# Eight of sixteen filter-spreading transfers on ScalarE's queue, and a new order, in a fused state-space convolution and gated MLP

## The chip, the cores and the metric

The kernel runs on one core of a Trainium2 chip. The metric is the device time of one execution, in microseconds; each kernel is run several times and the median is quoted. The profile is one execution taken by the hardware profiler, and its times count from the start of its span.

The engines are called by the profile's names: PE is TensorE (PEld its weight loads), DVE is VectorE, ACT is ScalarE, POOL is GpSimd, and SP is SyncE, which here does nothing but issue transfers.

## The reference, cut to what matters

The input `x` is 2048 positions by 640 channels. After a layer normalisation, `xn` goes through two branches, and the output is the sum of `x` and both.

```python
xn = layernorm(x)
# branch A: a long convolution per channel d, its filter K made from 128 complex modes n
P = exp(dt * (A_re + 1j * A_im) * l)                 # 640 x 128 x 2048
K = einsum('dn,dnl,dn->dl', C, P, dt * B).real       # 640 x 2048
y = irfft(rfft(pad(K)) * rfft(pad(xn.T)))[:, :2048].T + xn * Dskip
# branch B: gated MLP with a mixing over positions
z = gelu(xn @ w_in)                                  # 2048 x 1728
z1, z2 = z[:, :864], layernorm(z[:, 864:])
g = w_sp @ z2 + b_sp[:, None]                        # 2048 x 2048 times 2048 x 864
out = x + y + (z1 * g) @ w_out                       # 864 x 640
```

## The kernel before, in words

**Stages.** Everything is in one program, in which the two branches are interleaved.

- *Start (0 to about 90 us).* `x` and `w_in` are loaded. DVE and ACT normalise `x` into `xn`, which also goes to the DRAM buffer `xn_scratch`. PE makes `xn @ w_in` (tags `mm1b` and `mm1a`: 432-wide matmuls, ten for each of 32 row blocks), and ACT evicts each with a gelu. The second half of `w_in`'s columns (`WINB`) is used first. DVE computes the statistics of `z2`; each of the 16 `z2` blocks is then normalised either on ACT or on DVE.
- *Filter (about 90 to 200 us).* The class `Kgen` makes the filter `K` for 20 chunks of 32 channels (`NCH`, `CH`), in two parts of ten chunks. For each chunk PE makes phases (`kpe`), ACT turns them into sines in two instructions (tag `ktrig`, function `trig`), DVE multiplies magnitudes (`mags`) and products (`products`), and PE contracts them over the modes (`contract`, 64 small matmuls on 24 columns). `kg.trigs[c]` is the last sine instruction of chunk `c`; other work is tied to these. There are three buffers for the sines (`NTR`). Each part's magnitudes need exponentials on ACT (`exps`), which need another activation table than the sines. Between the chunks PE works at the mixing `w_sp @ z2` (`mm2`), whose `w_sp` tiles come by transposing transfers; DVE gates the result (`gate`), and it goes to the DRAM buffer `zg_scratch`.
- *Convolution (about 195 us to the end).* The class `Conv` transforms input and filter in two stages of matmuls (`stage1`, `stage2`), multiplies them on DVE (tag `pw`), and transforms back (`inverse1`, then `inv2`), once for each of the two parts. The input of the first transform, `TLU`, is loaded by `load_u` from `xn_scratch` in eight transfers of 320 KB. The large constant of the second stage is `C2`. In between and after it, PE does the last product, `mm3`, on tiles of `zg_scratch` that transposing transfers bring (tag `zgt`).

**The fill.** A part's filter lies in `K2` with the values that the reference's bf16 positions call for, and has to be spread into `TLK`, the operand of `stage1`. `expand` writes `K2` to the DRAM buffer `k2d_scratch` (four stores), reads back four larger pieces, and then 16 small ones of 20 KB: eight for positions kept exactly, eight for those rounded to two (`EXACT` and `HALVES`; line 1324). Twelve copies on DVE or ACT (tag `spread`) spread the rest. The fill is done twice, once for each part. All its transfers are on SP's queue.

**What sets the order.** The program is first recorded as a list of operations. `Builder.schedule` then places them one by one on their engines: it goes by estimated durations, by the length of the work that hangs on each operation, and by an added figure for each group of operations (`SHIFT`, a long table). Some copies may go to ACT or to DVE, and the planner picks. What results is a fixed order for each engine and each queue, with semaphore waits where operations touch the same memory. `B.after(op, earlier)` only keeps an operation from being placed before another; it puts no wait into the program. An engine, or SP's queue, does its list in order: what stands behind a waiting entry waits too. Where tiles lie in SBUF is another table (`OFFSETS`). Tiles that aren't needed at the same time overlap, and the overlap makes waits.

The lines that the change touches besides these tables:

```python
XOT = 10
WOT = 12
UOT = 14
    cv.load_const("c2", "C2", kg.trigs[17])
    cv.load_u([kg.trigs[UOT + m // 2] for m in range(8)])
            B.dma(WINB, winv[:, :, FH:FF])
```

So the eight loads of `load_u` are tied to the sines of chunks 14 to 17, `C2` to chunk 17, and `w_out` to chunk 12.

Of the kernel before, what the change touches and what calls it, by code (L numbers as in the profile page):

```python
# [65 lines left out]
class Builder:  # L66
# [304 lines left out]
    def dma(self, out, in_, q="sp", wait=()):  # L371
        nb = self._dma_bytes(out)
        run = min(self._run(out), self._run(in_))
        per = 0.077e-3 if min([128] + [a.ap[0][1] for a in (out, in_) if 'DRAM' not in str(a.space).upper()]) <= 32 and run > 2048 else 0.037e-3 if run < 6000 else 0.045e-3
        op = self._add(q, lambda e: e.dma_start(out, in_), [in_] + list(wait), [out], is_dma=True, dur=0.55, lat=nb / run * (10e-3 + per * run) / 16)  # L375
        op.late = self.late.get(self.tag, 0.0)
        op.npk = nb / run / 16
        return op
# [337 lines left out]
class Psum:  # L716
# [25 lines left out]
FF = 1728  # L742
FH = 864
# [8 lines left out]
CH = 32  # L752
# [17 lines left out]
XOT = 10  # L770
WOT = 12
UOT = 14
OUTQ = (("sp",) * 4,) * 4 + (("sp", "pool", "sp", "pool"), ("sp", "act", "sp", "act"))
SHIFT = [
    1461.6, -117.7, 5299.6, -320.3, 1656.3, -585.1, 1763.6, 26.1, 1267.1, 880.0, -633.4, -370.4, 42.1, -1405.2, -471.9, 240.0,
    254.6, 1219.7, 333.5, -1999.5, 1976.3, 2197.4, 40.4, -90.3, -103.2, 540.3, 3080.4, 42.1, 38.8, 2850.1, 556.2, -367.7, 67.3,
    5571.0, -530.7, 952.0, -24.5, 338.5, 6324.0, 537.2, 302.2, 180.6, -957.6, 1643.2, 16.8, 902.2, -1600.9, 605.1, -802.3,
    2031.4, -1306.0, -780.7, -671.9, 112.0, -3008.2, -525.0, 1040.2, 862.9, 1287.1, 984.6, 0.0, -64.7, -959.6, -9.0, -1054.5,
    -2630.8, -2537.1, -2991.9, -1011.8, -3926.2, -591.7, -6744.4, -9.0, 25.9, -7345.2, -1133.1, -9424.9, -1929.4, 627.4, -364.0,
    965.9, 496.7, 629.4, -110.8, -121.3, -759.7, -1177.4, 480.5, -1197.3, -3403.7, -447.7, 898.1, 1345.4, -2969.0, -1517.5, 0.0,  # L780
    -3435.2, -1369.8, -37.9, 6726.1, 1236.6, -140.5, 449.9, -632.2, 1096.4, 284.8, 301.9, 276.3, 842.6, 378.2, 12361.1, 2383.3,
    4141.9, 0.0, -1.6, -165.8, 1279.3, 48.4, 2124.7, 2354.1, 906.1, 2654.6, -806.7, -347.3, -1862.7, -471.1, -522.2, -1067.9,
    -415.0, 2743.0, 1234.3, -270.9, -752.3, 0.0, 229.7, -988.3, 1179.3, 2749.5, 422.5, -55.8, -40.7, -68.1, -811.0, 0.0, 1089.6,
    1757.0, 1526.0, 2103.2, -69.7, 626.4, -30.5, -3352.9, -188.7, 1862.3, -2385.7, -1180.5, -549.1, -5568.3, 3140.0, -636.8,
    -226.7, -4354.1, -17.8, -184.5, 53.9, -9607.2, -2.9, -5759.3, -1188.1, -260.2, 1.3, -657.7, -2203.7, -424.7, -732.5, -2.6,
    -1322.0, 1.1, -489.2, -2.2, -2.6, 92.4, 1408.5, -2763.9, -641.9, -12.6, 66.3, 2712.2, -1338.6, -449.1, 162.2, -1878.5,
    1052.8, 986.9, 0.0, -1173.7, -951.0, 1307.7, -89.6, 1382.7, -4152.3, 6.1, 942.4, -13.1, 0.0, 2750.8, -383.8, 450.2, -592.9,
    -1973.8, 1396.3, 341.7, -2846.0, -307.2, 2653.6, 1018.7, -127.0, 1161.5, -341.3, -0.2, -519.7, 0.0, -2933.3, 992.3, -2932.9,
    1285.4, 933.9, -233.4, -4592.7, 850.7, -588.8, -606.5, -1083.9, 863.2, -449.4, -1858.1, -1.0, -436.2, -541.3, 978.0, -8.2,
    153.5, 929.5, -4177.6, -1.0, -742.2, -810.7, -1914.2, -970.0, -4.6, 868.9, -5270.0, -0.1, 14.4, -364.3, 227.7, -3.8, 2351.5,  # L790
    996.3, -6118.5, 1072.5, -4920.9, -10.5, 989.9, 2108.7, -4207.9, 19.9, -650.3, -2.3, 1697.9, 812.0, -48.7, 16.3, 0.0, -316.5,
    964.2, 2.4, 5.1, 12756.5, 413.6, -63.9, -29.5, -247.6, 12.2, 1000.8, 11416.5, -1091.2, 3120.4, 0.0, 219.7, 4899.7, -1039.5,
    -18.9, 4401.0, -2120.8, -14.1, 3471.9, 134.1, 1185.1, 7.0, 61.4, 7.0, -458.7, 67.2, 1741.9, 3459.0, 68.9, 1615.7, -607.8,
    -48.2, 1376.1, -152.7, 1791.3, 1014.0, 0.0, -1221.0, -500.9, 146.5, 7270.1, 231.7, -225.5, -476.5, -1970.4, 4833.2, -1016.4,
    76.0, -958.1, 206.8, -1937.6, 247.3, 0.0, 5.1, -3306.0, -1829.8, 196.8, 1528.0, 578.8, 1283.1, -501.8, -1621.3, 2897.0,
    7359.7, 1164.5, 3170.6, 9585.4, 696.7, 1828.4, 62.5, 2076.9, 1961.4, 1622.8, 3367.0, 2213.6, 1983.8, 16237.3, 2883.0,
    3106.7, 2690.4, 5604.1, 3820.4, 2156.5, 2325.2, 6606.1, 4254.2, 17981.2, 7.3, 5268.5, -674.7, -197.5, 2.0, 275.0, 8441.8,
    1305.0, 7453.6, 1391.6, 5133.7, 6281.3, 1384.9, 0.0, -324.3, 4083.8, 6831.6, 1385.9, 645.6, 430.0, 2533.1, -2947.5, 1282.5,
    807.3, -985.8, 2140.1, 1551.5, 464.9, -32.2, 3938.7, -84.9, -667.9, 190.1, 1220.1, 1192.0, 565.5, 1690.5, -869.4, 595.3,
    -704.9, 1174.8, -126.1, 11.4, 2116.3, 0.0, -997.8, 3517.0, 61.0, 1088.4, 1.6, 209.1, 10.9, -2456.1, -7207.6, -1631.5,  # L800
    -2836.8, -1735.7, -1533.6, -2236.7, 2.0, -1781.5, 1615.3, -2828.3, 1612.6, 1.8, 498.8, -3860.5, 4550.3, 416.1, 1572.6,
    -200.4, 881.8, -129.8, 319.4, -635.6, -45.7, -1084.3, 684.5, -830.4, -904.9, 58.0, -5231.7, -9.6, -70.8, 54.4, -1.7, 1.7,
    197.8, -193.2, -808.6, 39.4, -1904.6, -564.9, -1099.6, -21.6, -2289.8, -981.9, 957.2, 64.0, 5.7, 140.6, -1217.1, -166.9,
    10728.7, -230.1, 2524.4, 2209.7, 2255.4, 2580.2, -406.2, 1829.0, 972.4, 2954.1, 12199.2, 1506.0, 7180.5, 2130.2, 883.2,
    645.0, 6101.4, 1578.5, 847.9, -410.2, 3588.0, -2096.9, 4371.8, 5289.6, 1519.0, 2347.8, 1268.9, 98.9, 1.7, 2484.5, 3068.8,
    1414.5, 1969.4, 1062.7, 2271.3, 1196.4, 2147.0, 11592.3, 1106.4, 2144.0, 3679.9, -496.8, -7.5, 251.2, 17.1, -12.1, 153.6,
    769.9, 2667.8, 2251.3, -1391.0, 980.8, 996.5, 1113.4, 1225.2, -647.7, -349.9, 1919.7, -565.0, -129.2, -3495.3, -838.1,
    1603.9, -2605.8, -2855.8, 3148.0, -1020.3, 177.0, -2319.3, -4039.8, -3072.6, 531.6, 2401.0, 325.9, -3196.0, 1351.6, -2042.4,
    -3195.4, 2784.7, 1092.8, -260.7, -3300.8, -1668.5, -0.7, -28.4, -5227.0, 785.7, 23.5, 13.4, 0.0, 1159.2, 391.1, 8974.4,
    991.1, 965.3, -7163.2, -49.9, -844.4, 455.0, 96.6, 1.8, -2806.9, -328.1, -295.1, -18.8, -1970.3, -95.4, 1187.4, 102.0,  # L810
    -561.1, 62.5, -3884.6, -261.6, -5032.3, -332.0, -878.8, 207.4, -2.9, -728.4, -89.8, 62.0, 337.2, 0.0, 3155.1, 1202.6,
    3304.3, -211.8, 1376.2, 1544.4, 4613.0, 1618.6, 855.2, 1948.7, 2402.5, 1219.8, -1015.0, 2111.1, 3970.0, 7.0, -1728.5,
    1520.9, -194.9, -327.8, -2723.9, 1962.7, -1508.7, 1013.1, 2968.0, 117.0, -1067.3, 857.2, -3517.0, -397.6, -2125.0, -2912.3,
    1654.7, -50.0, 1368.4, -188.2, -716.4, 1993.7, 1409.8, -17.9, 1083.9, -465.4, 52.4, -105.8, -981.2, -2476.5, 989.7, 0.7,
    -112.8, 1859.9, -218.8, 1528.8, 2260.2, 283.0, -1286.4, -561.2, -2070.2, 510.3, -819.9, 220.5, 43.5, 146.7, -2443.4, 1339.6,
    -2363.1, -970.2, -4841.4, -878.2, -3598.7, -1020.2,
# [9 lines left out]
NTR = 3  # L826
NF = 3
# [3 lines left out]
    "BSB": 0, "RS2": 0, "Tpp": 0, "WOUT": 0, "YT0": 0, "NM2": 64, "ONE": 64, "MV2": 128,  # L831
    "WAV0": 256, "LDP": 320, "DTB": 384, "ST2": 1536, "MV": 1664, "RS": 1792, "NM": 1856, "YT1": 1920,
    "CEXP": 2560, "ST": 2624, "Twim": 2624, "WAV1": 2624, "LDT": 3392, "IDENT": 5184, "TAL1": 5440, "DTP": 6720,
    "TAL0": 8960, "XO": 8960, "Ttr": 10240, "WDP": 10240, "Tw2": 15360, "Twre": 17920, "MF": 19200, "UP0": 19200,
    "RG": 20736, "Tt4": 21312, "WS1": 21312, "XN": 21312, "Tt3": 23872, "Tth": 26432, "UP1": 29440, "TR2": 29504,
    "PC": 31552, "GT0": 34752, "K20": 38976, "RAW": 41792, "WS0": 44288, "Twab": 51456, "TR1": 52480, "RF": 57728,
    "X": 59520, "Z2": 60160, "V2": 70400, "CI": 87808, "KB0": 88320, "WINB": 88320, "WS2": 90240, "LFG0": 98432,
    "TLU": 98432, "Z": 98432, "PLB1": 108672, "KB2": 118912, "Y1K0": 118912, "Y1U0": 118912, "Y1K1": 120832, "Y1U1": 120832,
    "LFG1": 124672, "MG": 132352, "WINA": 132352, "TR0": 134464, "BSP": 141312, "K21": 141376, "PLB0": 141376, "KB1": 145600,
    "TLK": 147520, "XNT": 157376, "WS3": 157760, "C2": 165952, "DSKM": 178240, "W1U": 178560, "Z1": 179072, "GT1": 207744,  # L840
    "W1": 211968,
}
# [940 lines left out]
```

## Time and profile before

Before: 350.3 us, the median of three runs (348.77 to 352.11). The profiled span is 348.8 us.

| Engine | busy us | share of the span |
|---|---|---|
| PE | 317.8 | 91% |
| DVE | 263.2 | 75% |
| ACT | 229.2 | 66% |
| POOL | 17.9 | 5% |

A row of the windows (first us, last us, length) gives each engine's busy time and count of instructions in that stretch; PEclk is the share of full clock that TensorE was granted, and the DMA share is the mean busy share of the core's 16 DMA engines. It can pass 1 because packets overlap. A row of the waits gives who waited for whom, the total in us, how often, and the longest. A row of a timeline merges like instructions in sequence: start, time from the first to the last, and in brackets the idle time before them with its releaser. Rows with "q" behind the engine's name (SPq) are the issuing of transfers, and their time is the queue's, not the transfer's.

### The profile page before, as it was taken

The page shows a single profiled execution, that of the slowest core. Times are in us where ns is not written, and L with a number is a line of the kernel's source. Part 1 is how long each engine was busy: PE and PEld are TensorE (multiplying, and loading weights), DVE is VectorE, ACT ScalarE, POOL GpSimd, SP SyncE. Part 2 cuts the span into 40 slices and gives each one's busy share as a digit, 9 for nine tenths or more (in the row PEclk, how much of TensorE's full clock was granted, in tenths as well). Part 3 has the DMA queues.
Part 4 walks back from the last instruction along what each step waited for, and adds up shares of the span by engine and source line. Part 5 has one row for each costly group of instructions (what it writes and reads, how often), then busy time and mean ns, then how long its engine had stood idle before and what let it go on. Part 6 is the DMA issues. An engine that isn't in the chain of part 4 may idle for free.

```text
span 348.8 us, 9905 instructions
## 1 busy us (share of the span) xinstructions
PE 317.8 (91%) x4282; PEld 214.1 (61%) x4282; DVE 263.2 (75%) x502; ACT 229.2 (66%) x266; POOL 17.9 (5%) x34
## 2 busy tenths in 40 slices
PE   3899998999999999999999399999959999999972
PEld 2454566766466555565656267776638877659862
DVE  5998999998699998389899726649933396883282
ACT  3579984799566679875697127838835877446541
POOL 4111000211100000000000000000000200000001
PEclk9999999999999999999999969999998999999975
DMA  7994566454991647678999998896344869200047
GB/s 213 391 341 157 83 194 167 110 106 93 166 172 45 105 89 118 112 187 188 85 60 136 141 276 201 171 189 112 64 71 116 178 133 214 84 3 2 2 109 197
DMA packets 101700, 48.67 MB, mean 140 GB/s; under 512 B 82137, under 2 KB 99514, under 8 KB 101146
## 3 DMA queue, kind: packets, MB, share of 16 engines
q1 hardware_dynamic: 100824, 45.07, 63.0%
q0 software_dynamic: 448, 2.79, 4.1%
q8 instruction: 33, 0.54, 0.7%
q10 hardware_dynamic: 386, 0.20, 0.2%
q14 instruction: 9, 0.07, 0.1%
HBM read 18.47 MB, written 11.61 MB: 86 GB/s over the span
## 4 chain that ended last, share of the span: by engine, by line
PE 56%; SPq 14%; ACT 13%; DVE 7%; DMA 5%; issue 2%; POOL 0%; POOLq 0%; DVEq 0%
PE ps L341 55%; SPq L375 11%; ACT arena L263 10%; DVE arena L273 4%; ACT L263 3%; SPq L382 3%; DMA arena<-xn_scratch 2%; DMA arena<-in_B_w_in_dram 2%; DVE arena L1099 1%; DVE arena L285 1%; DMA arena<-zg_scratch 1%; DVE arena L304 1%; PE ps L348 0%; DVE ps L297 0%; DVE arena L280 0%
## 5 line engine op out<-in xcount | busy, mean ns | idle before, releaser
L341 PE MATMUL ps<-arena 128*24 128x33 bf16 (+11 forms) x4222 | 314.6, 269 | 22.9 <-DMA arena<-xn_scratch 6.1
L341 PEld LDWEIGHTS ps<-arena 128*128 128x128 bf16 (+5 forms) x4222 | 210.0, 114 | 124.1 <-issue 25.3
L263 ACT ACTIVATE arena<-ps 128x1024 bf16<-128x1024 f32 (+6 forms) x184 | 173.8, 972 | 108.4 <-PE ps L341 97.6
L273 DVE TENSOR_TENSOR arena<-arena 128x128 bf16<-128x128 bf16 (+12 forms) x199 | 121.2, 646 | 13.4 <-ACT arena L263 10.5
L304 DVE CAST arena<-ps 128x1024 bf16<-128x1024 f32 (+2 forms) x28 | 32.5, 1171 | 25.5 <-PE ps L341 21.2
L273 DVE TENSOR_TENSOR arena<-ps,arena 128x320 bf16<-128x320 f32 (+3 forms) x42 | 22.9, 561 | 23.7 <-PE ps L341 23.5
L263 ACT ACTIVATE arena<-arena 128x320 bf16<-128x320 f32 (+10 forms) x65 | 34.6, 590 | 3.3 <-DVE arena L273 2.9
L1513 DVE BATCH_NORM_STATS2 arena<-arena 128x6 f32<-128x320 bf16 (+1 forms) x64 | 30.1, 535 | 3.2 <-DMA arena<-in_A_u_dram 3.1
L285 DVE SCALAR_TENSOR_TENSOR arena<-ps,arena 128x432 bf16<-128x432 f32 x32 | 21.1, 662 | 11.3 <-PE ps L341 9.5
L263 ACT ACT_TABLE_LOAD x17 | 21.8, 1283 | 2.0 <-issue 1.8
L280 DVE TENSOR_SCALAR arena<-arena 128x544 bf16<-128x544 bf16 (+5 forms) x43 | 13.2, 317 | 1.0
L375 POOL DMA_DIRECT2D arena<-in_A_u_dram x8 | 4.1, 514 | 190.4 <-PE ps L341 183.2
L271 POOL TENSOR_TENSOR arena<-arena 128x4 f32<-128x4 f32 (+2 forms) x10 | 9.8, 977 | 62.1 <-DVE arena L280 62.1
L313 DVE TENSOR_SCALAR arena<-arena 128x864 bf16<-128x864 bf16 (+1 forms) x19 | 8.1, 479 | 0.1
L348 PE MATMUL ps<-arena 128*128 128x128 bf16 x60 | 6.0, 238 | 1.7 <-DVE arena L280 1.7
L348 PEld LDWEIGHTS ps<-arena 128*128 128x128 bf16 x60 | 4.6, 107 | 4.0 <-DVE arena L280 2.1
L304 DVE COPY arena<-arena 32x960 bf16<-32x960 bf16 (+4 forms) x14 | 4.6, 375 | 0.1
L285 DVE SCALAR_TENSOR_TENSOR arena<-arena 128x4 f32<-128x4 f32 (+4 forms) x14 | 4.6, 328 | 0.1
L375 POOL DMA_DIRECT2D out_dram<-arena x2 | 1.0, 501 | 70.6 <-DVE arena L273 70.6
L1099 DVE RECIPROCAL arena<-arena 128x640 f32<-128x640 f32 x1 | 4.2, 4153 | 0.0
L1515 DVE BATCH_NORM_AGGREGATE arena<-arena 128x2 f32<-128x12 f32 x32 | 3.9, 169 | 0.1
L304 DVE CAST arena<-arena 128x1280 bf16<-128x1280 f32 (+1 forms) x4 | 2.6, 660 | 0.1
(11 smaller groups left out, 6.5 us busy)
## 6 DMA issues: line engine op xcount, KB each, us to landing
arena<-arena SPq DMA_DIRECT2D x12, 360.0 KB, 6.2
zg_scratch<-arena SPq DMA_DIRECT2D x16, 216.0 KB, 2.4
xn_scratch<-arena SPq DMA_DIRECT2D x4, 640.0 KB, 5.5
arena<-in_A_u_dram POOLq DMA_DIRECT2D x8, 320.0 KB, 6.6
arena<-xn_scratch SPq DMA_DIRECT2D x8, 320.0 KB, 8.2
arena<-in_B_w_in_dram SPq DMA_DIRECT2D x2, 1080.0 KB
arena<-in_A_u_dram SPq DMA_DIRECT2D x3, 640.0 KB
out_dram<-arena SPq DMA_DIRECT2D x16, 120.0 KB, 2.1
```

Source lines behind the costliest of these rows:

```text
L263: return e.activation(out, in_, func, bias=bias, scale=scale)
L271: return self._add(q, lambda e: e.tensor_tensor(out, in0, in1, op), [in0, in1], [out], dur=d, port=True)
L273: return self._add(q, lambda e: e.tensor_tensor(out, in0, in1, op), [in0, in1], [out], dur=self._dve_cost("tt", out, [in0, in1]), port=port)
L280: return self._add(q, lambda e: e.tensor_scalar(out, in0, s1, s2, op0, op1), self._aps(in0, s1, s2), [out], dur=self._dve_cost("ts", out, ...
L285: return self._add("dve", lambda e: e.scalar_tensor_tensor(out, in0, scalar, in1, op0, op1), self._aps(in0, scalar, in1), [out], dur=self. ...
L304: "dve": (lambda e: e.tensor_copy(out, in_), self._dve_cost("ts", out, [in_]))}
L313: "dve": (lambda e: e.tensor_scalar(out, in_, scale, bias, ALU.mult, ALU.add), self._dve_cost("ts", out, [in_]) + 0.11)}
L341: op = self._add("pe", lambda e: e.matmul(out, lhsT, rhs, start=start, stop=stop, **kw), [lhsT, rhs], [out], dur=d)
L348: op = self._add("pe", lambda e: e.transpose(out, in_, ident), [in_, ident], [out], dur=0.09, lat=0.3)
L375: op = self._add(q, lambda e: e.dma_start(out, in_), [in_] + list(wait), [out], is_dma=True, dur=0.55, lat=nb / run * (10e-3 + per * run) ...
L382: return self._add(q, lambda e: e.dma_start_transpose(out, in_), [in_], [out], is_dma=True, xbar=True, dur=1.3 if nb < 400000 else 2.6, la ...
L1513: B.generic("dve", (lambda e, c=c: e.bn_stats(st[:, a, c, :], src[:, a, w * c:w * c + w])), [src[:, a, w * c:w * c + w]], [st[:, a, c, :]] ...
```

## The change

The eight small `HALVES` transfers of each fill are issued from ACT's queue (`EXQ`), so that SP's queue has fewer to issue. `load_u`, `C2` and `w_out` are tied to earlier chunks (12 to 15, 15 and 10). `WINB` is loaded in two halves, one for each half of a block's matmuls. The rows of the filter table run the other way, so that the pieces to be read lie at regular places; the magnitudes' plane order follows, and their last two small products become one of 192 and one of 64 elements in place of two of 128. The planner's estimates for a transfer's issue and for the time to landing of `load_u` change, and both tables (`SHIFT`, `OFFSETS`) are new, so that the order changes throughout. The two tables and the reordered constants are left out of the diff here.

```diff
-        op = self._add(q, lambda e: e.dma_start(out, in_), [in_] + list(wait), [out], is_dma=True, dur=0.55, lat=nb / run * (10e-3 + per * run) / 16)
+        op = self._add(q, lambda e: e.dma_start(out, in_), [in_] + list(wait), [out], is_dma=True, dur=0.66 if self.tag == "expand" else 0.57, lat=nb / run * (10e-3 + per * run) / 16)
...
+EXQ = "act"
+XOT, WOT, UOT, C2T = 10, 10, 12, 15
...
-ROWS = [2 * r for r in range(16)] + [0, 2, 0, 2, 0, 2, 4, 6]
+ROWS = [30 - 2 * r for r in range(16)] + [2, 0, 2, 0, 2, 0, 6, 4]
...
-EXACT = ((0, 0), (1, 16), (2, 20), (3, 18))
-HALVES = ((0, 2, 0), (1, 2, 0), (2, 22, 0), (3, 2, 1))
+HALVES = ((0, 12, 0), (1, 12, 0), (2, 22, 0), (3, 12, 1))
...
-        outer(mf[:, 16:20, :], f[:, F_AWF + 4:F_AWF + 6, :], f[:, F_BF:F_BF + 2, :], 2, 2)
-        B.tt("dve", mf[:, 20:24, :], f[:, F_BF:F_BF + 4, :], f[:, F_AWF + 6, :].unsqueeze(1).to_broadcast([128, 4, CH]), ALU.mult)
+        outer(mf[:, 16:22, :], f[:, F_AWF + 4:F_AWF + 7, :], f[:, F_BF + 2:F_BF + 4, :], 3, 2)
+        B.tt("dve", mf[:, 22:24, :], f[:, F_BF:F_BF + 2, :], f[:, F_AWF + 5, :].unsqueeze(1).to_broadcast([128, 2, CH]), ALU.mult)
...
-        for p0, r, n in ((32, 4, 16), (64, 8, 32)):
+        for p0, r, n in ((32, 8, 16), (64, 0, 32)):
...
-        for p0, where in ((0, [(d, r, 0) for d, r in EXACT]), (16, HALVES)):
-            for h in range(2):
-                for d, r, dc in where:
-                    B.dma(two(TL[p0 + 8 * h:p0 + 8 * h + 8, :], d * NB, [64 * NB, (4 * NB, 16), (1, NB)]),
-                          two(kd[4 * r:4 * r + 8, :], (16 * h + dc) * NB, [w, (NB, 16), (1, NB)]))
+        for h in range(2):
+            for d in range(4):
+                r = 14 + 2 * d
+                B.dma(two(TL[8 * h:8 * h + 8, :], d * NB, [64 * NB, (4 * NB, 16), (1, NB)]),
+                      two(kd[4 * r:4 * r + 8, :], 16 * h * NB, [w, (NB, 16), (1, NB)]))
+        for h in range(2):
+            for d, r, dc in HALVES:
+                B.dma(two(TL[16 + 8 * h:24 + 8 * h, :], d * NB, [64 * NB, (4 * NB, 16), (1, NB)]),
+                      two(kd[4 * r:4 * r + 8, :], (16 * h + dc) * NB, [w, (NB, 16), (1, NB)]), q=EXQ)
...
-    B.late = dict(uswap=2.5, uload=1.0, expand=5.0, zgd=3.0)
+    B.late = dict(uswap=2.5, uload=2.5, expand=5.0, zgd=3.0)
...
-            B.dma(WINB, winv[:, :, FH:FF])
+            for h in range(2):
+                B.dma(WINB[:, :, 432 * h:432 * h + 432], winv[:, :, FH + 432 * h:FH + 432 * h + 432])
...
-    cv.load_const("c2", "C2", kg.trigs[17])
+    cv.load_const("c2", "C2", kg.trigs[C2T])
```

## The prediction

> **What bounds the kernel now.** I read the page's busy times and chain, then the waits, the windows, and the timelines of the SP queue and DVE.
>
> ```profile
> PE 317.8 (91%) x4282; PEld 214.1 (61%) x4282; DVE 263.2 (75%) x502; ACT 229.2 (66%) x266; POOL 17.9 (5%) x34
> ...
> PE 56%; SPq 14%; ACT 13%; DVE 7%; DMA 5%; issue 2%; POOL 0%; POOLq 0%; DVEq 0%
> ```
>
> TensorE is busy 317.8 of 348.8 us, so at most 31 us can be had by filling its holes. The first 10 us (3.34 busy) and the last 6.8 us (0.43 busy) account for 13 of them. The chain puts 14% on SP's queue: for long stretches the issuing of transfers sets the end. The waits say where that reaches TensorE:
>
> ```profile
> PE ps L341 <- DMA arena<-xn_scratch: 6.1, 1, 6.1
> ...
> PE ps L341 <- DMA arena<-zg_scratch: 3.7, 3, 2.4
> ```
>
> Two places cost 9.8 us of the 22.9 us that line 341's matmuls idle. The windows show the first and what it brings with it (busy us of PE, PEld, DVE, ACT, POOL, then PEclk, DMA share, GB/s):
>
> ```profile
> 190.00:194.00 4.00, 4.00 (x88) 2.79 (x82) 3.76 (x9) 2.81 (x3) 0.00 (x0) 1.00 1.55 142
> 194.00:198.00 4.00, 1.25 (x7) 0.57 (x5) 3.84 (x9) 0.00 (x0) 0.00 (x0) 1.00 1.28 122
> 198.00:202.00 4.00, 0.64 (x3) 0.58 (x4) 0.33 (x1) 0.00 (x0) 0.00 (x0) 0.71 1.15 233
> 202.00:206.00 4.00, 4.00 (x74) 2.73 (x73) 0.00 (x1) 0.00 (x0) 0.00 (x0) 0.50 1.01 319
> ```
>
> PE falls from 4.00 to 1.25 and 0.64 busy, and the granted clock is 0.50 after it. The SP queue (start, length, count) gives the reason:
>
> ```profile
> 162.02 7.54 SPq L375 DMA_DIRECT2D arena<-k2d_scratch  x11
> 169.61 0.60 SPq L375 DMA_DIRECT2D arena<-xn_scratch  x1
> 170.25 4.46 SPq L375 DMA_DIRECT2D arena<-k2d_scratch  x4
> 174.75 0.58 SPq L375 DMA_DIRECT2D arena<-xn_scratch  x1
> 175.38 6.38 SPq L375 DMA_DIRECT2D arena<-k2d_scratch  x5
> 181.80 0.58 SPq L375 DMA_DIRECT2D arena<-xn_scratch  x1
> 182.42 3.51 SPq L382 DMA_TRANSPOSE arena<-in_B_w_sp_dram  x2
> 185.98 10.74 SPq L375 DMA_DIRECT2D arena<-xn_scratch  x5
> 196.76 2.35 SPq L375 DMA_DIRECT2D arena<-c_c  x1
> ...
> 244.99 11.15 SPq L375 DMA_DIRECT2D arena<-k2d_scratch  x16
> 256.18 3.86 SPq L382 DMA_TRANSPOSE arena<-zg_scratch  x3
> ```
>
> TensorE waits for the eight xn_scratch loads (`load_u`, the input of the first transform). They stand among 16 small filter transfers that cost 0.59 to 0.66 us of issue each (11 in 7.54 us), so the queue reaches the last five only at 186. Then they go at 10.74 / 5 = 2.1 us apiece, at a DMA share of 1.30 to 1.55: from there the transfers limit, not the issue. The second fill of 16 takes 11.15 us at 245, and the zg_scratch transposes that `mm3` needs stand behind it. TensorE's hole there:
>
> ```profile
> 256.00:260.00 4.00, 1.50 (x11) 0.81 (x9) 0.36 (x1) 1.05 (x2) 0.00 (x0) 1.00 0.50 76
> 260.00:264.00 4.00, 2.77 (x12) 1.69 (x13) 0.98 (x2) 0.00 (x0) 0.00 (x0) 0.64 0.46 143
> ```
>
> Removing a hole isn't worth its whole length, since DVE's last filter products end at 198.3:
>
> ```profile
> 195.15 3.18 DVE L273 TENSOR_TENSOR arena<-arena 128x1536 bf16<-128x1536 bf16 x6
> ```
>
> **What the Trainium skill says.** "DMA: Bandwidth & Descriptors", section "Issuing engines are not separate DMA queues": all issuers feed the same 16 DMA engines, and a second issuer saves only sequencer time. The trace agrees that issue is a real price here (0.66 us against transfers of 20 KB), and that it's the only thing to save once the share is over 1. "TensorE: Matmul & The Clock Gate", section "Part 1: The HAM clock gate": an idle window of about 3.4 us halves the clock, until about 3.4 us of work restore it. Here the clock reads 0.50 at 202 to 206 and mean 0.64 at 260 to 264, each after a hole. The same page's table has ScalarE as a strict FIFO: whatever waits at its head holds all behind it. No run here shows that yet for transfers in mid-kernel.
>
> **The change, part by part.** Orders are those of the built programs; the instruction counts of the engines together are the same except where said.
>
> *Eight of 16 spreads of each fill to ScalarE's queue.* SP is spared 8 x 0.66 = 5.3 us, twice. ScalarE pays 8 x 0.5 to 0.66 (its two output issues took 0.96 us, so 0.48 each; SP's median is 0.655): 4 to 5.3 us. I take 5.
>
> *Loads tied to earlier steps.* The order moves the u loads from chunks 14 to 17 of the filter to 12 to 15, and C2 from 17 to 15. In the new SP order the first fill's stores still wait for chunk 9's evacuation, 146.4 before. After them come four stores 2.3, two zg stores 1.1, w_out 1.2, one transpose 1.3, six w_sp transposes 6 x 1.3 = 7.8: the first u load is at about 160. Twelve k2d reads take 12 x 0.66 = 7.9, to 168; seven u loads at the DMA rate, 7 x 2.1 = 14.7, to 183. The last lands 8.25 us after its issue (as before): about 189 against 201.2. TensorE wants it at 195: hidden, with 6 us of margin. C2 waits for chunk 16's magnitudes on DVE (its space is now part of theirs), which is past by then. Behind it on SP stand ten w_sp transposes and the second k2d store. C2 issued at 183 to 185 took 8.6 us to land before: 194, first used after the first-stage matmuls, about 202. The ten transposes drain after it, and `mm2` wants them from about 200: thin, up to 1 us may show.
>
> *First hole.* Gone are 6.1 us and up to half of the 5 us worked at half clock (2.5). But the last filter contraction can't start before DVE is done at 198.3; only the other work moves up. At 209 TensorE was back at full pace; I put that point at 202: -7. Bounds: -4 (only what precedes 198.3, with the clock half) and -8.6.
>
> *Second hole.* Before, the `mm3` groups stand close together, and wait for zgt transposes one at a time. The new order puts the fill (8 x 0.66 = 5.3) ahead of 15 of the transposes, but spreads `mm3` out: most matmuls on the second set of transposes now stand among those of the inverse's first stage. Gone: 3.7 and half of about 3 us at half clock (1.5): -5. Bounds -2 and -5.2.
>
> *ScalarE in the chunk loop.* It takes 10 of the first 12 spread copies, 6 before: four more of about 1.0 us (32x960 took 1005 ns), and the 5 us of issue, between its sines of chunks 13 to 19. Between 160 and 195.2 it was busy 6.23 + 8.16 + 11.29 = 25.7 of 35.2 us. Now 25.7 + 4 + 5 = 34.7: full. The gaps it fills are those in which it waited for the phases in PSUM, and queued behind each issue are sines for which DVE's products wait. DVE loses four copies (4 x 0.4 = 1.6) there and has sines in hand (three buffers). I take +1; bounds 0 and +5.
>
> *w_in halves.* One more issue (0.47) and runs of 864 bytes. PE started at 10.35 after 1.32 us of waiting for it; its other input was copied at 9.76: -0.5, and nothing if the later x loads slip.
>
> *The rest.* The reversed rows change addresses only. In the magnitudes 40 products of 128 elements (219 ns) become 20 of 192 and 20 of 64; with the slope between the 512 and 1056 rows (421, 704 ns: 0.52 ns an element) 252 + 186 = 438 = 2 x 219: nothing. ScalarE takes four more z2 normalisations (1106 ns; 497 on DVE): +4.4 us against -2.0 in a stage where each is over 80% busy; with 27 `mm2` matmuls fewer ahead of the first full phase block (27 x 0.18 = 4.9 us, the same work later as filler), between -2 and +2: 0. Activation table loads stay 17.
>
> Sum: -7 - 5 + 1 - 0.5 = -11.5, and +0.5 for the thin wait: -11. 350.3 - 11 = 339.3, say 339.
>
> **Rivals.**
> *Only the second hole goes (346).* For: DMA share is over 1 from 170 on, and issue moved to another queue makes no transfer faster; if the ScalarE transfers keep the engines busy just when the u loads start, these land at 195 to 200 again. Against: they're 20 KB each, the share was 0.75 at 166 to 170, and the loads now start 10 us earlier in the order. 350.3 - 5 + 1 - 0.5 = 345.8.
> *ScalarE becomes the bound (355).* For: it's full by my count. If its issues stall as SP's did [...] (2.64 us at most, 2.1 mean for the u loads), 8 cost 17 us, not 5, and the loop grows by these 12; if the second fill's 5 us delay the evictions of the first stage too, less the 1 us or so that a spare buffer hides, +4: 350.3 - 11 + 12 + 4 = 355. Against: separate queue, small transfers, three sine buffers.
> *More than the holes (331).* Chunk loop starts up to 5 us earlier because of the 27 matmuls, DVE is done before 195, and TensorE's last 14 us (two waits of 0.47 and 1.64 us, clock 0.71) are filled by the `mm3` matmuls now put between the output groups: 350.3 - 11 - 5 - 3 = 331.
>
> **How the numbers follow.** Main 0.58, only the second hole 0.16, ScalarE 0.11, more 0.15. The same-band is 346.8 to 353.8. Main and more give faster, 0.73; of the second rival's 0.16, 0.07 is faster and 0.09 within; ScalarE's 0.11 I split 0.04 within and 0.07 slower: 0.80, 0.13, 0.07, and for what I can't see in a whole new order I move 0.02 from faster to slower. Low end 331; high end 349 leaves out most of the ScalarE case.
>
> **What would show it.** First hole: TensorE's wait for xn_scratch under 1 us, the last u load landed before it's wanted, no half clock near the end of the chunks. Second: zg_scratch waits near 0. ScalarE: 16 k2d issues at 0.5 to 0.7 us each; if they take over 1 us, or DVE's waits for ScalarE grow from 10.5 us by more than 3, that rival is right. If TensorE waits instead for w_sp or C2, the thin place was the wrong side. If TensorE's holes are gone and the time isn't, the chunk loop got longer for a reason that I haven't named.

## The result, and the profile after

The kernel after took 339.4 us (median of 4 runs, 338.1 to 342.7) beside 349.7 us for the kernel before (with a fourth run): 0.971 of it, 95% interval 0.962 to 0.980. Run once more among the experiments it gave 0.965 (0.960 to 0.970). The prediction was 339.0. Its profiled span is 337.6 us, 11.2 less than before. One profile among the experiments, of the kernel with only the second fill on SP, is of a slow execution (346.1 us, where that kernel's fast ones took 337.8 to 341.7), so nothing rests on its sizes alone, and all ratios compare fast executions.

The first rows of the page's busy times and of its chain, kernel after:

```profile
PE 314.9 (93%) x4282; PEld 210.1 (62%) x4282; DVE 264.4 (78%) x501; ACT 230.4 (68%) x267; POOL 17.7 (5%) x34
...
PE 71%; ACT 9%; DVE 7%; DMA 5%; issue 2%; ACTq 2%; SPq 2%; POOL 1%; POOLq 0%; DVEq 0%
```

SP's queue has fallen from 14% of the chain to 2%, and PE's own work fills 71% of it instead of 56% (6% and 65% in a second profile of the same kernel). The waits of the kernel after (who waited for whom, total, times, longest):

```profile
ACT arena L263 <- issue: 15.4, 2, 10.0
...
PE ps L341 <- ACT arena L263: 5.5, 6, 2.4
...
PE ps L341 <- DMA arena<-xn_scratch: 0.4, 1, 0.4
```

There is no row for zg_scratch any more, and the 0.4 us for xn_scratch lies ahead of 80 us, at the first projection: the u loads cost TensorE nothing. New are ScalarE's 15.4 us in two waits, and TensorE's wait for ScalarE has grown from 2.8 to 5.5 us. SP's timeline (start, length, issues) answers to the one shown of before:

```profile
155.83 1.22 SPq L375 DMA_DIRECT2D arena<-xn_scratch  x1
157.22 9.94 SPq L375 DMA_DIRECT2D arena<-k2d_scratch  x12
167.19 14.39 SPq L375 DMA_DIRECT2D arena<-xn_scratch  x7
181.69 2.69 SPq L375 DMA_DIRECT2D arena<-c_c  x1
184.43 16.29 SPq L382 DMA_TRANSPOSE arena<-in_B_w_sp_dram  x10
```

The last u load was issued at 193.0 before, and at 179.7 now. ScalarE's and TensorE's timelines show what it cost (in brackets the idle time ahead, with its releaser):

```profile
156.50 6.50 ACTq L375 DMA_DIRECT2D arena<-k2d_scratch  x8
163.04 1.45 ACT L263 ACTIVATE arena<-ps 128x1536 bf16<-128x1536 int16 x1 [5.48 <-issue]
...
222.71 7.59 ACTq L375 DMA_DIRECT2D arena<-k2d_scratch  x8
230.40 0.73 ACT L263 ACTIVATE arena<-arena 64x640 bf16<-64x640 bf16 x1 [9.96 <-issue]
```

```profile
139.68 48.12 PE L341 MATMUL ps<-arena 32*128 32x384 bf16 x804
188.15 41.62 PE L341 MATMUL ps<-arena 128*128 128x432 bf16 x501 [0.35 <-DVE arena L285]
232.17 40.10 PE L341 MATMUL ps<-arena 64*128 64x160 bf16 x503 [2.39 <-ACT arena L263]
```

The first block of issues holds ScalarE's sines by 5.48 us, and TensorE doesn't notice: its row runs from 139.68 to 187.80 (139.68 + 48.12) without a wait. The second block holds the evictions of the filter's second transform, and TensorE stands for 2.39 us. The windows (PE, PEld, DVE, ACT, POOL, clock, DMA share, GB/s) show the clock after it:

```profile
232.00:236.00 4.00, 3.83 (x45) 2.20 (x47) 3.00 (x4) 2.89 (x4) 0.00 (x0) 0.63 1.48 133
236.00:240.00 4.00, 4.00 (x43) 2.62 (x41) 3.10 (x3) 2.69 (x3) 0.00 (x0) 0.94 0.25 26
```

The clock after the old holes, kernel before (the window from 260 us stands in the prediction):

```profile
200.00:204.00 4.00, 2.64 (x41) 1.86 (x45) 0.00 (x0) 0.00 (x0) 0.00 (x0) 0.50 0.94 334
204.00:208.00 4.00, 4.00 (x118) 2.79 (x107) 1.56 (x2) 1.03 (x1) 0.00 (x0) 0.69 1.60 281
264.00:268.00 4.00, 4.00 (x48) 3.81 (x47) 2.34 (x2) 2.89 (x3) 0.00 (x0) 0.94 0.47 98
```

Most of the 11.2 us can be summed from these rows. The waits at the two old holes: 6.1 + 3.7 = 9.8 gone. Clock lost after holes, reckoned as (1 - clock) x 4 us over these windows: before 2.0 + 1.2 (200 to 208 us) and 1.4 + 0.2 (260 to 268), now 1.5 + 0.2: 3.1 gone. TensorE's waits for ScalarE take back 5.5 - 2.8 = 2.7. Together 10.2; where the last 1 us lies isn't shown. Such a count is rough. It leaves out the end, where the clock is low in both kernels (0.52 from 336 to 340 us before, 0.58 from 328 to 332 now), and a hole can be worth less than its wait and its lost clock, as the account of the prediction shows for the new one.

### The profile page after: what moved, and what is told of

It is laid out like the page before. It is cut to its first block, busy times and chain, and to the rows that moved or that the text cites. A ratio compares the mean times of both kernels' runs of the same rounds, so it can differ in the third digit from the quotient of the medians.

```text
span 337.6 us, 9918 instructions
## 1 busy us (share of the span) xinstructions
PE 314.9 (93%) x4282; PEld 210.1 (62%) x4282; DVE 264.4 (78%) x501; ACT 230.4 (68%) x267; POOL 17.7 (5%) x34
## 4 chain that ended last, share of the span: by engine, by line
PE 71%; ACT 9%; DVE 7%; DMA 5%; issue 2%; ACTq 2%; SPq 2%; POOL 1%; POOLq 0%; DVEq 0%
PE ps L341 71%; ACT arena L263 6%; DVE arena L1516 3%; ACT L263 3%; DMA arena<-in_A_u_dram 3%; ACTq L375 2%; DVE arena L273 2%; SPq L382 1%; DMA arena<-xn_scratch 1%; DMA xn_scratch<-arena 1%; DVE arena L280 1%; SPq L375 1%; POOL arena L271 0%; DVE arena L285 0%; DVE arena L313 0%
## 5 line engine op out<-in xcount | busy, mean ns | idle before, releaser
L341 PE MATMUL ps<-arena 128*24 128x33 bf16 (+10 forms) x4222 | 311.8, 268 | 14.7 <-ACT arena L263 5.5
L341 PEld LDWEIGHTS ps<-arena 128*128 128x128 bf16 (+5 forms) x4222 | 206.2, 115 | 116.4 <-ACT arena L263 22.5
L263 ACT ACTIVATE arena<-ps 128x1088 bf16<-128x1088 int16 (+8 forms) x181 | 170.8, 975 | 89.5 <-PE ps L341 68.2
L273 DVE TENSOR_TENSOR arena<-arena 128x512 bf16<-128x512 bf16 (+14 forms) x199 | 121.5, 646 | 10.2 <-ACT arena L263 6.8
L304 DVE CAST arena<-ps 128x1024 bf16<-128x1024 f32 (+3 forms) x32 | 35.5, 1116 | 20.3 <-PE ps L341 19.8
L263 ACT ACTIVATE arena<-arena 128x320 bf16<-128x320 f32 (+8 forms) x69 | 39.6, 626 | 10.6 <-issue 10.0
L285 DVE SCALAR_TENSOR_TENSOR arena<-ps,arena 128x432 bf16<-128x432 f32 x32 | 21.2, 666 | 14.1 <-PE ps L341 13.9
L313 DVE TENSOR_SCALAR arena<-arena 128x864 bf16<-128x864 bf16 (+1 forms) x15 | 6.4, 476 | 0.1
L304 DVE COPY arena<-arena 32x640 bf16<-32x640 bf16 (+4 forms) x13 | 4.2, 368 | 0.1
L304 DVE CAST arena<-arena 128x640 bf16<-128x640 f32 (+1 forms) x5 | 3.0, 622 | 0.0
```

The lines of the kernel that those rows point to most:

```text
L263: return e.activation(out, in_, func, bias=bias, scale=scale)
L273: return self._add(q, lambda e: e.tensor_tensor(out, in0, in1, op), [in0, in1], [out], dur=self._dve_cost("tt", out, [in0, in1]), port=port)
L285: return self._add("dve", lambda e: e.scalar_tensor_tensor(out, in0, scalar, in1, op0, op1), self._aps(in0, scalar, in1), [out], dur=self. ...
L304: "dve": (lambda e: e.tensor_copy(out, in_), self._dve_cost("ts", out, [in_]))}
L313: "dve": (lambda e: e.tensor_scalar(out, in_, scale, bias, ALU.mult, ALU.add), self._dve_cost("ts", out, [in_]) + 0.11)}
L341: op = self._add("pe", lambda e: e.matmul(out, lhsT, rhs, start=start, stop=stop, **kw), [lhsT, rhs], [out], dur=d)
```

## The experiments

In all of them, the edit comes after the planner has placed everything, and all that it doesn't name keeps the order of the kernel named. Most change only the queue of some transfers; the others merge two loads, set reads later, or hold loads back. To name them, `expand` marks the eight `HALVES` reads of fill `i` with `half = i`. Ratios are to the kernel before, run beside them on the same chip.

**Both parts of the change apart, and each fill apart.** The edit is one of these, at the end of `schedule`:

```diff
         order.sort(key=lambda o: (o.t0, o.gidx))
+        for op in order:
+            if op.tag == "expand" and getattr(op, "half", None) in (0, 1):   # or (0,) or (1,)
+                op.q = "sp"      # in the kernel after; "act" in the kernel before
```

*Old order, both fills on ScalarE's queue.*

> The kernel before with every engine's order kept, but the eight spreading reads of each fill issued by ScalarE: the second queue without the new order. My theory: SP is spared 5.3 us ahead of the last five u loads, which then begin at about 181 instead of 186, so that the xn_scratch wait shrinks from 6.1 to about 2 us; the second hole (zg_scratch 3.7 us) shrinks by most of it; ScalarE pays 8 x 0.8 us twice, of which 2 to 4 us reach TensorE. Time 343 to 347 us. Rival one (the queue does it all): 339 to 341 us. Rival two (the queue costs ScalarE as much as it spares SP): 349 us or more, with TensorE or DVE waiting for ScalarE instead.

It took 0.979 (0.975 to 0.983), 342.5 us. The u loads' wait is gone altogether, not down to 2 us, and so is TensorE's wait for zg_scratch (a weight load still waits 0.3 us). But ScalarE's issues now stand among the late sines. Its TensorE timeline:

```profile
174.70 2.52 PE L341 MATMUL ps<-arena 32*128 32x384 bf16 x22 [0.16 <-ACT arena L263]
180.52 10.69 PE L341 MATMUL ps<-arena 32*128 32x272 bf16 x175 [3.29 <-ACT arena L263]
```

The loop is held for 3.29 us, with the clock at 0.58 from 180 to 184. This also makes TensorE come later to the u loads, which is a part of why it doesn't wait for them. So the queue alone brings about 7 of the 10 to 12 us (0.971 and 0.965 for the whole change) and pays for it: my theory, with a time just under the range expected.

*New order, all sixteen on SP.*

> The kernel after with every engine's order kept, but all sixteen spreading reads issued by SP again: the new order without the second queue. My theory: the new order alone closes the first hole. The seven u loads begin at 167 + 8 x 0.7 = 173 instead of 167, the last lands at about 194 instead of 188, just when TensorE wants it: a wait for xn_scratch of 0 to 2 us; ScalarE gets back 6.5 us at 156 and 7.6 us at 223. Time 335 to 339 us. Rival: the queue is what closed the holes; the xn_scratch wait comes back with 4 us or more and a half clock after it, zg_scratch too, and the time is 345 us or more (before 350, after 339.4).

0.983 (0.979 to 0.987), 343.8 us: between theory and rival. The waits:

```profile
PE ps L341 <- DMA arena<-zg_scratch: 3.3, 3, 2.5
...
PE ps L341 <- DMA arena<-in_B_w_sp_dram: 1.9, 2, 1.0
...
PE ps L341 <- DMA arena<-xn_scratch: 1.2, 1, 1.2
```

The 1.2 us for xn_scratch lie ahead of 80 us again. The new order alone therefore keeps TensorE from waiting for the u loads, as I thought. It doesn't keep the second hole closed, and the ten w_sp transposes behind the loads come late instead. Alone, the order brings about 6 us and the queue 7, together 10 to 12: they overlap.

*New order, the first fill on SP, the second on ScalarE.*

> The kernel after with every engine's order kept, but the first fill's eight reads issued by SP again (the second fill's stay with ScalarE). My theory: in the new order the first hole is closed by the earlier u loads, and the first fill's queue is worth only what was seen ahead of 205 us in the run with both fills on SP, 1 to 2 us of waits for xn_scratch and w_sp; the last zg_scratch store still comes ahead of GpSimd's loads, so no zg_scratch wait: 0.967 to 0.973 of before (338 to 340 us), the 2.4 us wait for ScalarE at about 233 as in the kernel after. Rival: the first fill's queue is worth the whole difference of the two runs with the second fill on SP (0.983 against 0.972); then 0.976 or more.

0.975 (0.970 to 0.979), 341.6 us. SP's and TensorE's timelines:

```profile
158.11 14.28 SPq L375 DMA_DIRECT2D arena<-k2d_scratch  x20
172.43 14.43 SPq L375 DMA_DIRECT2D arena<-xn_scratch  x7
186.97 3.07 SPq L375 DMA_DIRECT2D arena<-c_c  x1
190.08 15.06 SPq L382 DMA_TRANSPOSE arena<-in_B_w_sp_dram  x10
```

```profile
203.97 0.37 PE L341 MATMUL ps<-arena 128*128 128x432 bf16 x1 [0.83 <-DMA arena<-in_B_w_sp_dram]
205.36 0.37 PE L341 MATMUL ps<-arena 128*128 128x432 bf16 x1 [1.03 <-DMA arena<-in_B_w_sp_dram]
206.67 28.91 PE L341 MATMUL ps<-arena 128*128 128x432 bf16 x286 [0.93 <-DMA arena<-in_B_w_sp_dram]
```

Twenty reads take 14.28 us where twelve took 9.94, and all behind them moves by about 5 us: the u loads still land in time, but `mm2` waits three times for w_sp, 2.8 us, with the clock at 0.59 from 206 to 210. I had counted the waits of the other run and not the clock: the time lies between theory and rival. So what the first fill's queue buys in the new order is the w_sp transposes, not the u loads. The interval overlaps that of the kernel after's first measurement and touches the second's, so the time that it buys isn't sharply known.

*New order, the second fill on SP, the first on ScalarE.*

> The kernel after with every engine's order kept, but the second fill's eight spreading reads issued by SP again (the first fill's stay with ScalarE). My theory: the second block holds ScalarE 7.6 us (222.7 to 230.3) and brings TensorE the 2.4 us wait at 232 and 3.4 us at half clock, 4.1 us in all; on SP the eight cost 8 x 0.7 = 5.7 us at about 241, ahead of the zg_scratch transposes, and these have that slack because their matmuls were spread out. So the wait for ScalarE at 232 goes, no zg_scratch wait returns, and the time is about 335.5 us (before 350, after 339.4). Rival one: SP's shorter queue is what closed the second hole; then zg_scratch waits of 3 us or more come back with a half clock behind them, and the time is 339 to 342. Rival two: the hole at 232 comes from a late first stage and not from the issues; the wait stays and the time is 339.5.

0.972 (0.967 to 0.976), 339.7 us by this ratio: the wait at 232 is gone (0.34 us), but TensorE waits for zg_scratch further on, as rival one says, in the new order with its spread-out `mm3`. My theory was wrong. The time itself can't be told from the kernel after's. In this kernel's own profile (the 346.1 us execution) the waits come to 6.5 us. The run with both fills on SP shows the same hole, in an execution of 342.4 us:

```profile
273.86 0.31 PE L341 MATMUL ps<-arena 128*128 128x320 bf16 x1 [2.50 <-DMA arena<-zg_scratch]
274.52 0.31 PE L341 MATMUL ps<-arena 128*128 128x320 bf16 x1 [0.35 <-DMA arena<-zg_scratch]
275.25 46.91 PE L341 MATMUL ps<-arena 128*128 128x320 bf16 x632 [0.42 <-DMA arena<-zg_scratch]
```

It differs from the run with only the first fill on SP in the second fill's queue alone, and that one has no such wait. SP's timelines, with both fills and with the first fill on SP:

```profile
236.18 11.24 SPq L375 DMA_DIRECT2D arena<-k2d_scratch  x16
...
260.14 0.59 SPq L375 DMA_DIRECT2D zg_scratch<-arena  x1
267.02 9.28 SPq L382 DMA_TRANSPOSE arena<-zg_scratch  x7
```

```profile
238.37 5.67 SPq L375 DMA_DIRECT2D arena<-k2d_scratch  x8
...
256.65 0.59 SPq L375 DMA_DIRECT2D zg_scratch<-arena  x1
259.12 11.56 SPq L382 DMA_TRANSPOSE arena<-zg_scratch  x7
```

The last zg_scratch store goes out 3.5 us later, but the transposes that wait for it start 7.9 us later: 6.9 us after the store instead of 2.5. GpSimd issues four loads of 320 KB of the residual input at 255.7 with both fills on SP, ahead of the store, and at 260.7 with the first fill on SP, behind it. With only the second fill on SP the store goes out at 259.7, behind the loads (254.5), and the transposes start 10.2 us after it. So in the new order SP's shorter queue is what keeps the second hole closed.

**The first projection's weights in one piece.** The kernel after with the two halves' operations merged after planning:

```diff
+        one.emit = whole       # one transfer of all 864 columns
...
+        order.remove(two)      # what waited for two waits for one
```

> The kernel after with every engine's order kept, but the second half of the first projection's weights loaded by one transfer instead of two. My theory: TensorE's first matmul of the projection (8.78 us) starts about 0.5 to 1.5 us later, and because the stage after it is set by other loads and by DVE, at most 0.5 us of it reaches the end: 339.4 to 340. Rival: the halves are worth the whole head start, 1.3 us or more: 340.7 us.

0.965 (0.961 to 0.968), as the kernel after run again: the halves are worth nothing that can be measured. TensorE waited 1.1 us for w_in, against 0.7 and 0.4 in the two profiles of the kernel after.

**Can the price on ScalarE be saved?** First the zero point:

> The kernel after once more, beside the other three of this call, as their zero point: 337 to 340 us, with the 2.1 to 2.4 us wait for ScalarE at 232 and no zg_scratch wait.

0.965 (0.960 to 0.970), with a wait of 2.54 us at 232.7. Then the second fill's reads later on ScalarE and in pieces:

```diff
+        mine = [op for op in order if op.tag == "expand" and getattr(op, "half", None) == 1]
+        for op in mine:
+            order.remove(op)
+        ev = [op for op in order if op.tag == "ev2k" and op.q == "act"]
+        for at, n in ((1, 4), (3, 2), (5, 2)):      # n reads behind that eviction
+            k = order.index(ev[at]) + 1
+            order[k:k] = mine[:n]
+            mine = mine[n:]
```

> The kernel after with its second fill's eight reads still on ScalarE, but not as one block ahead of the evictions of the filter's second transform: four behind the first two of these evictions (where ScalarE idled 4.3 us in the run with that fill on SP), two behind the fourth, two behind the sixth. My theory: TensorE's hole at 232 comes from the block standing ahead of the evictions in ScalarE's queue; with it gone, and SP's queue short as in the kernel after, the 2.4 us wait and the 1.7 us lost at half clock both go and no zg_scratch wait comes: about 4 us under the kernel after, 333 to 336 us. Rival: the issues hold up the evictions wherever they stand; two or three smaller waits for ScalarE come in its place and the time is the after's, 337 to 340 us.

0.966 (0.960 to 0.971): no gain. The hole at 232 is gone without smaller waits in its place, so the time is the rival's, but not for the rival's reason. TensorE's timeline shows where the gain went:

```profile
231.45 4.66 PE L341 MATMUL ps<-arena 64*128 64x160 bf16 x69 [0.34 <-DVE arena L304]
236.30 35.05 PE L341 MATMUL ps<-arena 128*128 128x256 bf16 x440 [0.19 <-ACT arena L263]
273.16 45.57 PE L341 MATMUL ps<-arena 128*128 128x320 bf16 x632 [1.81 <-DMA arena<-zg_scratch]
```

TensorE reaches the `mm3` matmuls at 271.35, 0.9 us ahead of the kernel after (272.27), waits 1.81 us for zg_scratch and goes on at 273.2 as the other does (273.19). Here the last store went out at 256.11, just behind GpSimd's loads (255.44), and the transposes began at 263.26.

Both fills on GpSimd's queue, which issues nothing between 86 and 257 us, in both orders:

```diff
+            if op.tag == "expand" and getattr(op, "half", None) in (0, 1):
+                op.q = "pool"      # with more DMA semaphores for that queue
```

> The kernel after with every engine's order kept, but the sixteen spreading reads issued by GpSimd, which runs nothing between 86 and 257 us. My theory: neither SP's nor ScalarE's queue pays, so both holes stay closed and the one at 232 goes: 333 to 336 us; GpSimd's issues take about 0.5 us each as its u loads do. Rival: GpSimd's transfers go another way (its u loads took 8.0 us to land against 6 to 7 on SP) and are late, or slow DVE's copies [...]: TensorE waits for k2d_scratch reads or DVE's busy time grows by 3 us or more, and the time is 338 us or more.

> The kernel before with every engine's order kept, but the sixteen spreading reads issued by GpSimd: the second queue without the new order and without a price on ScalarE. My theory: the xn_scratch wait shrinks from 6.1 us to under 1 and the zg_scratch wait goes, as with ScalarE's queue, but the 3.3 us wait for ScalarE's sines at 180 that ScalarE's issues brought doesn't come: 2 to 3 us under that run's 342.3, 338 to 341 us. Rival: that wait came from elsewhere in the old order; the time is 342 us or more.

In the new order 0.969 (0.964 to 0.974), in the old one 0.976 (0.971 to 0.981). GpSimd issued eight in 5.4 and 5.8 us and DVE's busy time stayed (264.7 against 264.4 us); the wait for ScalarE at 232 is gone. Yet the new order gains nothing over ScalarE's queue, against my theory: SP's twelve reads now took 13.15 us, TensorE waited 0.8 us for w_sp and 0.6 for zg_scratch. The time is the rival's, but neither of its signs is there. The old order came out near the upper end of the 338 to 341 us expected (340.6). The 3.29 us wait for ScalarE at 180 isn't there, as expected, but 1.3 us of the wait for the u loads and 1.0 of zg_scratch stay, where I expected under 1 and none. Whether GpSimd's queue is better than ScalarE's in this order (0.976 and 0.979) the intervals don't say.

**GpSimd's loads held.** Three of these kernels with GpSimd's last four loads made to wait for the last zg_scratch transpose:

```diff
...
+            order.insert(order.index(zgt) + 1, op)
+            op.deps = op.deps + [zgt]      # op: the four loads, zgt: the last transpose
```

> The kernel with the second fill's eight reads back on SP, and in addition GpSimd's last four loads of the residual input (1.28 MB) held until the last zg_scratch transpose has landed. My theory now: SP's 5.7 us more of issue alone isn't what opened that run's 6.5 us of waits for zg_scratch; it pushed the last zg_scratch store from 253.3 to 259.7, behind GpSimd's loads, which were issued at 254.5 and fill the same DMA engines, so that the store took 10.2 us until the transposes could go instead of 2.4. With the loads held back the transposes start at about 262 instead of 270, the waits for zg_scratch fall to 1.5 us or less, and the time falls from that run's 0.972 of before to 0.957 to 0.963. Rival: the issue is the cause; the waits stay at 4 us or more, and the time at 0.969 or more.

> The kernel with the second fill's reads set later and in pieces on ScalarE, and in addition GpSimd's last four loads held until the last zg_scratch transpose has landed. My theory: that kernel closed the hole at 232 and lost the gain again at 273, since its last zg_scratch store (256.1) came behind GpSimd's loads (255.4) and the transposes started 7.1 us after it; with the loads held, the 1.8 us wait for zg_scratch goes, and the time is 0.953 to 0.960 of before (333 to 335 us). Rival: TensorE waits for ScalarE or DVE there instead; 0.964 or more.

> The kernel with both fills' spreading reads on GpSimd's queue, and in addition GpSimd's last four loads held until the last zg_scratch transpose has landed. My theory: no queue that TensorE waits for pays for the spreads now; zg_scratch waits of 0.6 us go too; 0.955 to 0.962 of before, as good as or better than any so far. Rival: that kernel's time (0.969) has another cause than the late transposes, such as the first projection of loads or GpSimd's way of issuing; 0.966 or more.

0.968 (0.964 to 0.972), 0.965 (0.960 to 0.970) and 0.969 (0.965 to 0.973). All of TensorE's zg_scratch waits are gone, and the transposes start 2.5 us after the store in all three. SP's timeline of the first:

```profile
231.42 12.00 SPq L375 DMA_DIRECT2D arena<-k2d_scratch  x16
...
255.68 0.59 SPq L375 DMA_DIRECT2D zg_scratch<-arena  x1
258.17 9.40 SPq L382 DMA_TRANSPOSE arena<-zg_scratch  x7
267.67 14.63 SPq L375 DMA_DIRECT2D arena<-arena  x8
```

So the collision was real, and 16 reads on SP were borne without waits once it was gone. This run doesn't prove it of the queue by itself, since SP was 3.7 us ahead when it came to the reads (231.42, against 235.08 without the hold), for a reason that I don't know. Nor is the time clearly better: 0.968 without these waits against 0.972 with them, and the intervals overlap. The time fell short of my theory in all three. The `uswap` transfers (arena<-arena) that come next now run beside the loads, and their issue takes 14.1 to 14.6 us instead of 10.9. In the second kernel TensorE ran through to 317.03, 2.6 us ahead of the kernel after, and then waited 1.20 us at the last stage, with the clock at 0.74 and 0.83 until 324. None of these versions beats the kernel after by more than the interval. What the last stage lacks there wasn't tried.

The store and the loads in eight profiles (us; the last column is from the last zg_scratch store's issue to the first transpose that waits for it; the last row is of the 346.1 us execution):

| kernel | store issued | GpSimd's loads | store to transposes |
|---|---|---|---|
| before | 260.7 | 271.8 | 2.4 us |
| after | 253.3 | 257.3 | 2.5 us |
| after, first fill on SP | 256.7 | 260.7 | 2.5 us |
| after, loads held, second fill on SP | 255.7 | 269.7 | 2.5 us |
| after, both fills on GpSimd | 256.8 | 256.6 | 4.5 us |
| after, both fills on SP | 260.1 | 255.7 | 6.9 us |
| after, second fill late | 256.1 | 255.4 | 7.2 us |
| after, second fill on SP | 259.7 | 254.5 | 10.2 us |

In the six other profiles the loads come behind the store too, and the transposes follow it by 2.4 to 2.5 us. In the kernel before, the loads came 11 us too late to collide: its second hole was the block of 16 reads on SP (11.15 us), with the transposes directly behind it.

## Why the prediction was right, point by point

*First hole, -7.* Right in place and way, too small in size: 6.1 us of wait and 3.2 of clock are gone, 9.3 by this count, beyond the far bound of 8.6. SP's times were guessed 4, 1 and 1 us late (160, 168, 183; they are 155.8, 167.2, 181.6). The price of 0.59 to 0.66 us an issue fits the first eleven reads; the nine that stood between the u loads before took 4.46 + 6.38 us, 1.2 each. Two causes overlap: the queue alone closes most or all of this hole in the old order, and the new order, with the earlier ties in it, closes it without the queue. That the last products on DVE would hold it to -7 was wrong: DVE was done at 193.8 instead of 198.3.

*The thin place, +0.5.* The w_sp wait was 0 and 0.3 us, but the place is as thin as I said: with eight more reads ahead of it, 2.8 us and a low clock.

*Second hole, -5.* Right in size (3.7 of wait and 1.6 of clock), and half right in its reason. That the block of reads on SP made this hole in the kernel before is borne out. But I let the spread-out `mm3` carry the rest and took SP's 5.3 us as no more than a help. With the fill on SP and the same `mm3` order the hole is back, at 3.3 us (6.5 in the other run). There it has another cause, which the prediction never looked at: the last store then goes out behind GpSimd's loads. SP's shorter queue brings it out ahead of them. With the loads held, the spread-out `mm3` bore 16 reads on SP.

*ScalarE, +1.* The first block cost about what was reckoned of ScalarE (5.48 us) and nothing of TensorE, and DVE's waits for ScalarE fell from 10.5 to 6.8. The issues took 0.81 and 0.95 us each, not 0.5 to 0.66. The second block, which I charged only in a rival, is the mis-sized term: 2.39 us of wait and 1.7 of clock, where I had 0 in the sum. The Trainium skill's strict FIFO (page "TensorE: Matmul & The Clock Gate", the table's row on queue depths) is now shown for transfers: the evictions waited behind the whole block. ScalarE stood idle for 9.96 us, 2.3 of them until a matmul released the first of the eight issues and 7.6 for the issues. For TensorE the hole is worth less than its 4.1 us: from its start (229.77) to the `mm3` matmuls it took 42.50 us, and 40.24 in the run with the reads set later (from 231.11), which shows no gain at the end. The prediction also reckoned with an idle window of about 3.4 us before the clock falls. Here the wait of 2.39 us was enough, and one of 2.06 us in the run with the weights in one piece (clock 0.57 from 232 to 236): the measurement decides.

*w_in halves, -0.5.* Not measurable. *The rest, 0*: not tried apart.

That the sum came out at -11 is in part luck: by this count the first hole gave 2.3 us more than I said, and the second fill's block on ScalarE, which wasn't in the sum, took about 3 back. The rival "only the second hole goes" is refuted by the missing wait for u loads. "ScalarE becomes the bound" describes the old order with the new queue (3.29 us and half clock at 180), not this kernel. "More than the holes" was half right: the chunk loop starts 4.1 us earlier (first sine at 85.5 instead of 89.6) and DVE was done 4.5 us earlier, but the last sine comes only 1.2 us earlier (191.4 instead of 192.6), and the tail stayed as long as before.

## What to carry to other kernels

When a queue that only issues transfers is on the chain, look what stands behind each block of small issues, and further down what will collide with it: here a store that went out 3.5 us later released its readers 7.9 us later, because it fell behind another engine's 1.28 MB of loads. Another engine's queue is a cheap place for issues where the work behind them has slack (the sines at 156 us in the new order: nothing of TensorE), and a dear one where it has none (the late sines in the old order: 3.29 us; the evictions: 2.39 us). And a hole's length is not its worth: of seven versions that closed the hole at 232, none was measurably faster than the kernel after. In some the next wait took its place; in the others what did isn't known.

## What was not expected of the hardware

A 216 KB store that released its readers within 2.5 us of its issue took 4.5 to 7.2 us (10.2 in the 346.1 us execution) when 1.28 MB of loads, issued from another engine, were ahead of it; the loads' own queue didn't keep them apart. The Trainium skill ("DMA: Bandwidth & Descriptors", section "Issuing engines are not separate DMA queues") has it that all issuers' transfers run on the same 16 engines; the table above is that, with numbers.

A second issuer wasn't free to the first. In the two profiles in which SP issued all twenty reads of the first fill alone, the first twelve took 8.6 and 8.7 us. Where ScalarE issued eight at the same time, SP's twelve took 9.5 to 11.5 us in seven profiles (9.94 in the kernel after's). With GpSimd's eight issued ahead, SP's twelve took 13.15 and 14.12 us, but nearly all of the excess is one issue, the first. Its row for the shorter one (times of one issue in ns: least, median, most):

```profile
L375 SPq DMA_DIRECT2D arena<-k2d_scratch x12: 593/655/5570, 157.2 to 169.7; - x12
```

Whether the issues or the transfers meet there wasn't settled.
